# A transformer block on one core: first two key products in five parts, eight initial warm-up products, two x tiles ahead of the key weights, and new orders

## The chip, the cores and the metric

The program runs on one core of a Trainium2 chip. The core has TensorE (PE in the profile, with its weight loads as PEld), VectorE (DVE), ScalarE (ACT), GpSimd (POOL) and SyncE (SP), which here only issues DMAs. The metric is the device time of one execution in microseconds (us). Matrix products write to PSUM, which this kernel divides into four buffers of two banks each; everything else lives in SBUF.

## The reference

The input x has 2,048 rows of 640 features in bfloat16. It is normalised, goes through linear attention with 32 heads of 20 features, and then through a dense layer with 1,728 hidden features. Cut to what matters:

```python
q, k, v = split(layernorm(x) @ wqkv)                # 32 heads of 20
pq, pk  = q @ w_phi, k @ w_phi                      # per head, 20 x 20
phi_q   = concat(softmax(pq), softmax(-pq))         # 40 features; phi_k likewise
kv, z   = sum_s phi_k * v, sum_s phi_k              # over all rows
o       = (phi_q @ kv) / (phi_q @ z + 1e-6)
h       = x + o @ wo
out     = h + silu(layernorm(h) @ w1) @ w2
```

## The kernel before

The rows are cut into 16 tiles of 128 rows (t = 0 to 15). The work is written as some 620 small steps, each a Python function `op_..`, and the text `ORDER` (lines 25 to 67) lists them one after the other as words: `kp.3.0.3` calls `op_kp(3, 0, 3)`. Each engine runs its own steps in the order of this text; semaphores make it wait for what it reads and for buffers that it overwrites. Each engine takes its instructions strictly in order, so a step that waits holds up all later steps of the same engine. A DMA is issued by SP or ACT, as the last letter of its word says (`s`, `a`); a copy or product by DVE, ACT or POOL (`v`, `a`, `p`).

The steps at the start, with the lines of the profile:

- `lx.a.b`, `lk.a.b`, `lv.a.b` (L220) load tiles a to b of x, and 128-row chunks a to b of the five of the key weights wk and of the value weights wv; `lp` loads w_phi. One tile or chunk is 160 KB. `l1`, `l2`, `lh`, `lo` load the weights of the dense layer and of the output.
- `wm.n` (L254) is a product of a constant tile with n columns whose result nobody reads. Six of 512 columns stand ahead of `ORDER`, and two more stand in it.
- `wt.c` (L302) transposes wk chunk c on PE in five instructions, and `wc.c` copies it out of PSUM (L160 on DVE, L162 on ACT). `ph` (L190) spreads w_phi over a block diagonal. `fk.c` (L317) multiplies the two in six products, and `fc.c` (L162) casts the result into chunk c of Wfk: key weights with w_phi folded in.
- `st.t` (L260) takes a tile's statistics, `rs` and `rm` (L265, L269) make the scale and shift, `xn.t` (L277, L282) normalises. Tiles 0 to 3 are transposed on PE (`xt`, L288) and copied (`xc`), the others by a DMA transpose (`xd`, L295).
- `kp.t.a.b` and `vp.t.a.b` (L347) are the key and value products of tile t over chunks a to b of the five; each chunk takes two products of 320 columns. Without a and b all ten are made.
- `lq.c` (L235) loads a chunk of the query weights transposed by DMA, into the buffer that held wk, so after all `wt` have read the part that it overwrites; `gk.c` (L317) and `gc.c` fold w_phi into it.

Then `ke` (exponentials, L368), `kr` (sums, L376) and `ka` (normalisation, L384, on POOL) finish each tile's keys, `vc` casts its values, and `cc` (L406) adds them into one PSUM buffer that is held for the whole stage. `qp` and `qe` (L426, L436) make the queries. After `close`, tile by tile, `dp` (L459), `dw`, `dr` and `do` (L494) make the output of the attention, `td` transposes it by DMA, `op` (L521) multiplies with wo, `oa`, `sq`, `sa`, `sr`, `hn` and `hd` normalise and transpose it again; `up` (L595), `ua` (L617) and `yp`, `yh`, `yq` (L641, L656) are the dense layer, and `yo`, `yz`, `so`, `sz` add x and store. There is no planner at run time: the order in the text is the order on the chip.

Of the kernel before, what the change touches and what calls it, by code (L numbers as in the profile page):

```python
# [30 lines left out]
xc.1.a rs.4.2 vc.2.a vp.1 xn.5.v xn.4.v xd.5 st.7 vp.0 vc.1.a st.8 xd.4 rs.6.2 vc.3.a gk.2 st.11
vc.0.a rm.7 kp.1 lq.0 ke.0 st.9 lq.4 vp.5 ke.1 st.10 xn.6.v vp.4 xn.7.a rs.8.4 st.12 xd.6 vc.5.a
st.13 kp.5 mo vc.4.a xd.7 gc.2.a st.14 kp.4 ke.5 lo.s rm.9 xn.11.v st.15 gk.4 xn.9.a gk.0 kr.3 kp.6
rs.12.4 gc.4.a xd.9 ke.4 vp.6 rm.14 lq.3 rm.13 xn.8.v ke.6 ka.3.p kr.1 vp.7 xd.11 gc.0.a gk.1 xd.8
xn.12.v vc.7.a ka.1.p kp.7 kr.2 xn.14.a xd.12 vc.6.a vp.9 xn.13.a xn.15.v ka.2.p kr.0 gc.1.a kp.9
xd.13 vc.9.a ke.7 vp.11 xd.15 xn.10.v ka.0.p kr.5 l2.4.8.s cc.1 l1.2.s cc.3 vc.11.a l2.0.4.s cc.2
kr.6 xd.14 ke.9 gk.3 ka.5.p kp.8 gc.3.a lh.s vp.13 kr.7 ke.8 l1.1.s ka.6.p xd.10 kp.12 vc.13.a kr.4
vp.12 ka.7.p kr.9 kp.15 vc.12.a ke.12 ka.4.p kp.13 kr.8 kp.11 ka.9.p kr.12 cc.5 cc.6 ke.15 cc.7 cc.0
cc.4 ka.12.p ke.11 kr.15 kp.14 ke.13 vp.15 kr.11 ka.15.p ke.14 vp.14 vc.15.a kr.14 vp.8 ka.8.p kp.10
vc.8.a kr.13 ka.14.p qp.0.0 ke.10 vc.14.a kr.10 qp.0.2 ka.13.p qe.0.0 vp.10 qe.0.2 ka.11.p qp.1.0  # L40
vc.10.a qp.0.1 ka.10.p qe.1.0 cc.15 qe.0.1 cc.9 cc.12 cc.11 cc.14 cc.13 cc.8 cc.10 qp.1.2 km.0 close
km.1 dp.1.0 qe.1.2 dp.1.1 qp.1.1 dw.1.v dp.0.0 qe.1.1 dp.0.1 dr.1 qp.2.1 dw.0.v dp.3.0 qe.2.1 dp.3.1
dr.0 qp.3.0 dw.3.v do.0.1.p do.0.0.p td.0 dp.5.1 qe.3.0 dp.5.0 dr.3 qp.2.0 dw.5.v l1.0.s do.3.0.p
do.1.0.p do.3.1.p do.1.1.p dp.4.0 td.3 qe.2.0 dp.4.1 dr.5 op.0 dw.4.v do.5.0.p td.1 do.5.1.p qp.2.2
oa.0 dp.2.1 qe.2.2 dp.2.0 dr.4 qp.3.2 dw.2.v do.4.1.p sq.0 do.4.0.p op.1 qe.3.2 sa.0 td.4 sr.0
dp.9.1 dr.2 dp.9.0 oa.1 op.3 td.5 hn.0 sa.1 sq.1 dw.9.v do.2.1.p hd.0 qp.3.1 sr.1 hn.1 op.4 oa.3
qe.3.1 hd.1 sa.3 op.5 do.2.0.p oa.4 td.2 sq.4 dp.10.0 dp.10.1 up.0.1 dw.10.v l2.8.13.s op.2 dr.9
ua.0.1 dr.10 do.9.1.p oa.5 do.10.0.p up.0.3 oa.2 do.9.0.v dp.6.1 ua.0.3 dp.6.0 dp.8.1 sq.3 dw.6.v
td.9 up.0.0 sq.2 sr.3 sq.5 sa.4 dp.8.0 sr.4 ua.0.0 up.0.2 dw.8.v sa.2 sa.5 op.9 dr.6 ua.0.2 hn.4
do.6.0.p hd.4 sr.5 yp.1.0 oa.9 sr.2 hn.3 hn.5 hd.3 dr.8 dp.7.1 dp.7.0 hn.2 do.8.1.p yh.0.0 do.8.0.v  # L50
yp.1.1 hd.5 do.10.1.p sa.9 hd.2 do.6.1.p yp.0.0 yo.1 dw.7.v yp.0.1 dr.7 dp.11.1 do.7.0.v do.7.1.p
dp.11.0 up.1.5 yo.0 td.7 dw.11.v td.8 up.1.6 ua.1.5 td.10 dp.13.1 ua.1.6 so.0 dp.13.0 up.1.2 td.6
dw.13.v dp.15.0 dp.15.1 up.1.1 dw.15.v op.8 ua.1.1 dr.11 sq.9 op.6 ua.1.2 op.7 oa.6 dr.13 sa.6 sq.6
do.11.0.v up.1.3 oa.7 sr.6 oa.8 do.11.1.v sa.8 up.1.4 ua.1.3 sa.7 do.13.1.p sq.8 sr.9 dp.12.0 ua.1.4
dp.12.1 up.1.0 hn.9 do.13.0.v sq.7 hd.9 dw.12.v sr.7 td.11 op.10 ua.1.0 td.13 hn.6 yp.3.0 oa.10 so.1
dr.15 hn.7 dr.12 dp.14.0 dp.14.1 do.12.0.p yh.1.1 dw.14.v yp.3.1 do.15.0.p do.12.1.p sa.10 td.12
yp.5.0 sr.8 dr.14 hd.6 yp.5.1 hd.7 op.11 yo.5 yp.4.0 oa.11 hn.8 sa.11 yo.3 hd.8 op.12 do.15.1.v
do.14.0.v td.15 op.13 oa.12 so.5 sq.12 up.2.2 so.3 sq.11 up.2.0 ua.2.2 op.15 ua.2.0 up.2.6 oa.15
oa.13 yh.1.0 do.14.1.v sq.13 up.2.1 td.14 sq.15 ua.2.6 yp.2.0 ua.2.1 up.2.5 up.2.4 ua.2.5 sq.10
sr.10 up.2.3 sr.11 sa.13 hn.11 yp.4.1 ua.2.3 sa.15 sa.12 ua.2.4 sr.13 op.14 yp.9.1 oa.14 hn.10 sa.14  # L60
sq.14 hd.10 sr.12 yp.9.0 sr.14 hn.12 yo.4 yp.2.1 sr.15 hn.13 so.4 hd.12 yp.8.1 yo.2 hd.11 so.2
yp.7.1 hd.13 yh.2.1 yh.2.0 yo.9 yp.8.0 so.9 yp.7.0 up.3.3 yo.7 hn.14 hn.15 hd.14 yo.8 up.3.4 ua.3.3
hd.15 so.8 yp.6.0 ua.3.4 up.3.0 up.4.3 yp.6.1 up.4.1 yo.6 so.6 so.7 up.3.2 ua.4.1 ua.3.0 up.3.5
ua.3.2 up.4.2 ua.3.5 up.4.0 ua.4.2 up.3.1 ua.4.0 ua.4.3 up.3.6 ua.3.1 yp.15.1 ua.3.6 yp.14.1 yp.10.1
yp.14.0 yp.12.1 yp.15.0 yh.4.0 yh.3.0 yp.12.0 yp.10.0 yo.12 yo.14 yo.15 yp.11.0 so.15 so.12 so.14
yp.11.1 yh.3.1 yq.13.0 yo.11 yo.10 so.11 so.10 yq.13.1 yz.13.0 yz.13.1 sz.13.0.s sz.13.1.a
"""

@with_exitstack
def kernel(  # L70
# [181 lines left out]
    def op_wm(n=512, ps=None):  # L252
        ps = mm2() if ps is None else ps
        nc.tensor.matmul(ps[:, 0, 0:n], warm[:, 0:P], warm[:, 0:n], start=True, stop=True)  # L254
        return ps
# [462 lines left out]
```

## Time and profile before

| | |
|---|---|
| Median of 3 runs | 240.59 us (239.21 to 241.1) |
| The profiled execution's own time | 240.93 us |
| Its span, first to last instruction | 239.0 us |
| Mean granted TensorE clock | 0.999 |
| PE busy | 232.8 us |
| HBM read, written | 9.61 MB, 2.62 MB |

The span begins with the program's first instruction and leaves out what the device does around it (1.93 us in this execution). Times in the views count from the span's start. A row of a view that groups instructions gives their count, their busy time and the mean of one; the text in `<-` names what ended the engine's idle time. Matrix products are pipelined, so the distance between two of them, not the duration of one, is what a product costs.

### The profile page before, as it was taken

Reading aid. Unit: us, or ns where it says so; the run is one execution under the profiler, and the core shown is the slowest. Engines: PE = TensorE matmul, PEld = TensorE weight load, DVE = VectorE, ACT = ScalarE, POOL = GpSimd, SP = SyncE. Lnnn points to the kernel's source line nnn. Section 1 sums busy time; section 2 is a strip of 40 time slices with the busy share of each in tenths; the row PEclk is TensorE's granted clock in tenths of the full one; section 3 lists DMA queues with packets and bytes.
Section 4 is the critical chain, followed back from the end, with each engine's and each line's share of the span. In section 5 each row is a group of like instructions: output and inputs, shape, how many; then the busy total and the mean of one; then the engine's idle time right before and its main releaser. Section 6 shows DMA issues by size and latency. Waiting matters only on the chain.

```text
span 239.0 us, 5196 instructions
## 1 busy us (share of the span) xinstructions
PE 232.8 (97%) x2140; PEld 151.5 (63%) x2156; DVE 130.6 (55%) x254; ACT 104.4 (44%) x154; POOL 90.8 (38%) x167
## 2 busy tenths in 40 slices
PE   6999999999999999999999999999999999999995
PEld 2977777777574456786656467655576556757662
DVE  3679999999408998786966584430042301000043
ACT  2677998656865674661035510244510113550000
POOL 6423599999950566348201641000550000000000
PEclk9999999999999999999999999999999999999999
DMA  6995596970000264615360054401046221000022
GB/s 170 369 191 126 114 204 114 352 191 0 3 3 3 38 170 88 185 32 76 45 133 0 2 110 82 110 3 27 1 29 139 55 58 55 0 3 0 0 85 82
DMA packets 42807, 20.60 MB, mean 86 GB/s; under 512 B 34336, under 2 KB 42272, under 8 KB 42784
## 3 DMA queue, kind: packets, MB, share of 16 engines
q1 hardware_dynamic: 41984, 20.21, 36.9%
q8 instruction: 17, 0.28, 0.5%
q10 hardware_dynamic: 800, 0.06, 0.3%
q14 instruction: 6, 0.05, 0.1%
HBM read 9.61 MB, written 2.62 MB: 51 GB/s over the span
## 4 chain that ended last, share of the span: by engine, by line
PE 95%; DMA 2%; ACT 1%; issue 1%; SPq 0%; DVE 0%
PE mm L641 24%; PE mm L595 24%; PE mm L347 18%; PE mm L426 9%; PE mm L521 9%; PE mm L459 3%; PE mm L406 3%; PE mm L317 2%; DMA wk<-in_A_wqkv_dram 2%; PE mm L605 1%; PE mm L656 1%; PE mm L302 1%; ACT EqT L436 1%; PE mm L288 0%; SPq L220 0%
## 5 line engine op out<-in xcount | busy, mean ns | idle before, releaser
L641 PE MATMUL mm<-w,shT 128*128 128x320 bf16 (+2 forms) x415 | 58.6, 299 | 0.2 <-issue 0.2
L595 PE MATMUL mm<-HnT,w 128*128 128x512 bf16 (+1 forms) x316 | 58.3, 335 | 0.4
L617 ACT ACTIVATE shT<-mm 128x1024 bf16<-128x1024 f32 (+2 forms) x29 | 27.6, 964 | 59.2 <-PE mm L595 53.8
L641 PEld LDWEIGHTS <-shT 128*128 128x128 bf16 x416 | 39.7, 98 | 18.0 <-issue 1.5
L595 PEld LDWEIGHTS <-w 128*128 128x128 bf16 x325 | 31.1, 98 | 23.1 <-issue 0.3
L664 DVE TENSOR_TENSOR ob<-mm,X 128x640 bf16<-128x640 f32 x15 | 12.1, 820 | 49.9 <-PE mm L641 43.4
L347 PEld LDWEIGHTS <-XnT 128*128 128x128 bf16 x320 | 30.9, 98 | 11.7
L384 POOL TENSOR_TENSOR Ek<-Ek,Sk 128x1280 bf16<-128x1280 bf16 x16 | 37.3, 2371 | 0.0
L494 POOL TENSOR_TENSOR o<-u,rd 128x320 bf16<-128x320 f32 x23 | 16.7, 748 | 24.0 <-DVE rd L488 11.8
L436 ACT ACTIVATE EqT<-mm 128x1024 bf16<-128x1024 f32 (+1 forms) x24 | 19.7, 880 | 11.6 <-PE mm L426 11.6
L347 PE MATMUL mm<-Wfk,XnT 128*128 128x320 bf16 x160 | 24.0, 299 | 0.0
L521 PE MATMUL mm<-wo,ot 128*128 128x320 bf16 x160 | 23.7, 299 | 0.0
L347 PE MATMUL mm<-wv,XnT 128*128 128x320 bf16 x160 | 23.7, 299 | 0.0
L376 DVE TENSOR_REDUCE Sk<-Ek 128x64 f32<-128x1280 bf16 x16 | 23.1, 1444 | 0.6 <-ACT Ek L368 0.6
L426 PE MATMUL mm<-XnT,Wfq 128*128 128x512 bf16 x94 | 22.9, 379 | 0.4
L368 ACT ACTIVATE Ek<-mm 128x640 bf16<-128x640 f32 x32 | 20.3, 718 | 4.4 <-PE mm L406 2.7
L538 ACT ACTIVATE sq<-X 128x640 bf16<-128x640 bf16 x16 | 11.7, 734 | 20.6 <-DVE X L530 20.5
L530 DVE SCALAR_TENSOR_TENSOR X<-mm,X 128x640 bf16<-128x640 f32 x16 | 12.9, 814 | 14.4 <-PE mm L521 14.3
L521 PEld LDWEIGHTS <-ot 128*128 128x128 bf16 x160 | 15.5, 98 | 6.8
L426 PEld LDWEIGHTS <-Wfq 128*128 128x128 bf16 x100 | 9.3, 98 | 10.4 <-issue 0.3
L560 DVE TENSOR_SCALAR hn<-X,HM 128x640 bf16<-128x640 bf16 x16 | 7.1, 456 | 15.1 <-POOL HM L554 15.1
L260 DVE BATCH_NORM_STATS2 stats<-X 128x6 f32<-128x320 bf16 x32 | 13.7, 469 | 2.1 <-DMA X<-in_A_x_dram 2.1
(69 smaller groups left out, 199.4 us busy)
## 6 DMA issues: line engine op xcount, KB each, us to landing
out_dram<-ob SPq DMA_DIRECT2D x15, 160.0 KB, 2.0
w<-in_B_w_dram SPq DMA_DIRECT2D x3, 720.0 KB, 6.5
X<-in_A_x_dram SPq DMA_DIRECT2D x3, 640.0 KB, 9.1
w<-in_B_w_dram SPq DMA_DIRECT2D x2, 640.0 KB, 6.5
wk<-in_A_wqkv_dram SPq DMA_DIRECT2D x5, 160.0 KB, 3.9
wo<-in_A_wo_dram SPq DMA_DIRECT2D x1, 800.0 KB, 6.2
w<-in_B_w_dram SPq DMA_DIRECT2D x1, 800.0 KB, 4.7
wv<-in_A_wqkv_dram SPq DMA_DIRECT2D x1, 480.0 KB, 7.9
```

The lines of the kernel that those rows point to most:

```text
L260: nc.vector.bn_stats(stats[:, k, :], X[:, t, k * 320 : (k + 1) * 320])
L347: nc.tensor.matmul(ps[:, half, 0:320], tok(XnT[t // GT], t)[:, c, :], W[:, c, half * 320 : (half + 1) * 320], start=(c == 0), stop=(c == C ...
L368: nc.scalar.activation(Ek[:, s, :].rearrange("p (a n) -> p a n", a=2), tl["kp", t][:, :, 0:320], AF.Exp, scale=1.0 - 2.0 * s,)
L376: nc.vector.tensor_reduce(Sk[:], tl["ek", t][:].rearrange("p s (h f) -> p (s h) f", f=DH), axis=AX.X, op=ALU.add,)
L384: eng.tensor_tensor(Ek3, Ek3, tl["sk", t][:, lo:hi].unsqueeze(2).to_broadcast([P, hi - lo, DH]), op=ALU.mult,)
L426: nc.tensor.matmul(ps[:, k, :], Wfq[:, c, r * P : (r + 1) * P], XnT[g][:, c, :], start=(c == 0), stop=(c == C - 1),)
L436: nc.scalar.activation(E[:, s, rs[0] : rs[-1] + 1, :], tl["qp", g, i][:, 0 : len(rs), :], AF.Exp, scale=1.0 - 2.0 * s,)
L494: (nc.vector if eng == "v" else nc.gpsimd).tensor_tensor(tl["o", t][:, a * 320 : (a + 1) * 320].rearrange("p (h f) -> p h f", f=DH), tl["u ...
L521: nc.tensor.matmul(ps[:, half, 0:320], tl["ot", t][:, c, :], wo[:, c, half * 320 : (half + 1) * 320], start=(c == 0), stop=(c == C - 1),)
L595: nc.tensor.matmul(ps[:, i * W : (i + 1) * W], w1[:, c, fc * P : (fc + 1) * P], HnT[g][:, c, 0:W], start=(c == 0), stop=(c == C - 1), skip ...
L617: nc.scalar.activation(sh[:, a:b], tl["up", g, k][:, 0 : b - a], AF.Silu)
L641: nc.tensor.matmul(ps, shT[g][:, fc * W + i * P : fc * W + (i + 1) * P], w2[:, fc, a:b], start=first and fc == 0, stop=last and fc == FC - ...
```

## The change

The six initial warm-up products become eight. In `ORDER`:

- x tiles 2 and 3 are loaded in one DMA ahead of the key weights; x tiles 1 and 0 are loaded one by one after the first part of the value weights. The chunks of the key weights come in the order 2, 0, 3, 1, 4 (before: 2, 1, 4, 0, 3).
- The key products of tiles 3 and 2, which were made in two parts (chunks 0 to 3 and 3 to 5), are made in five parts of one chunk each. The first part of tile 3's value products now comes ahead of its key products.
- One more filler (`wm.256`) stands in the order.
- The transposed loads of the query weights come in the order 4, 0, 3, 1, 2 and closer together; the load of x tiles 8 to 12 stands between them.
- Steps move between engines: the copies `wc.2` and `wc.0` from DVE to ACT and `wc.4` from ACT to DVE; `xn.7` and `xn.9` to DVE and `xn.6`, `xn.10`, `xn.11` and `xn.15` to ACT (with their `rm`), `xn.14` to DVE; half of the normalisation of tile 6 (`ka.6.h`, `kb.6`) and the cast `vc.14` to DVE; of the halves of `do`, five go from POOL to DVE and three from DVE to POOL. The last two stores swap their queues.
- The order of nearly all other steps is new as well. What they compute is the same, and no function is changed.

```diff
 ORDER = """
-lp.a lx.3.4.s ta lk.2.3.s lk.1.2.s mk lk.4.5.s lk.0.1.s ph.p lx.2.3.s st.3 lk.3.4.s wt.2 lx.0.2.s
-lv.0.3.s wt.1 rs.3 wc.2.v lv.3.5.s wt.4 wc.1.v wt.0 lx.4.8.s mc wc.4.a fk.2 xn.3.v lx.8.12.s fk.1
-wc.0.v fc.2.a st.2 wm.512 fk.0 fc.1.a wt.3 xt.3 fc.0.a lq.1 wc.3.v fk.4 rs.2 xc.3.v wm.256 fk.3
-fc.4.a kp.3.0.3 xn.2.v fc.3.a lq.2 st.0 xt.2 kp.3.3.5 xc.2.a lx.12.16.s st.1 vp.3.0.3 ke.3 kp.2.0.3
-rs.0.2 kp.2.3.5 xn.0.v vp.2.0.3 ke.2 xn.1.v st.5 xt.0 vp.2.3.5 xc.0.a st.4 vp.3.3.5 xt.1 kp.0 st.6
...
+lp.a lx.2.4.s ta lk.2.3.s lk.0.1.s mk lk.3.4.s lk.1.2.s lk.4.5.s lv.0.3.s ph.p lx.1.2.s st.3
+lx.0.1.s wt.2 lv.3.5.s st.2 wc.2.a rs.3 lx.4.8.s wm.512 wt.0 wm.256 wt.3 wc.0.a fk.2 wc.3.v rs.2
+wt.1 fc.2.a fk.0 xn.3.v fk.3 wc.1.v mc fc.0.a xt.3 fk.1 xc.3.v wt.4 fc.1.a xn.2.v wm.256 vp.3.0.3
+lq.4 wc.4.v fc.3.a st.1 mo xt.2 kp.3.0.1 lq.0 xc.2.a kp.3.1.2 kp.3.2.3 st.0 fk.4 vp.2.0.3 fc.4.a
+lx.8.12.s rs.0.2 lq.3 vp.3.3.5 kp.3.3.4 vc.3.a kp.3.4.5 xn.0.v vp.2.3.5 lq.1 xn.1.v ke.3 st.5
+kp.2.0.1 kp.2.1.2 xt.0 lh.s kp.2.2.3 st.4 xc.0.a kp.2.3.4 xt.1 vc.2.a kp.2.4.5 lq.2 kp.0 st.6 rs.4.2
+ke.2 xn.5.v vp.0 xc.1.a xn.4.v xd.5 st.7 ke.0 kp.1 st.11 lx.12.16.s rs.6.2 vc.0.a xd.4 st.8 vp.1
+ke.1 xn.7.v st.10 gk.2 xd.7 gk.0 gc.2.a vp.5 st.9 vc.1.a lo.s gc.0.a kr.1 gk.3 rs.8.4 kp.5 gc.3.a
...
-yp.11.1 yh.3.1 yq.13.0 yo.11 yo.10 so.11 so.10 yq.13.1 yz.13.0 yz.13.1 sz.13.0.s sz.13.1.a
+yo.11 so.15 so.11 so.9 yq.13.1 yz.13.0 yz.13.1 sz.13.0.a sz.13.1.s
 """
...
-        for i in range(6):
+        for i in range(8):
             ps = op_wm(512, ps)
```

More of the change, by code (lines that the diff above doesn't have):

```diff
@@ L31 @@
[L31 to L65, printed above, removed]
@@ new lines @@
+kp.2.0.1 kp.2.1.2 xt.0 lh.s kp.2.2.3 st.4 xc.0.a kp.2.3.4 xt.1 vc.2.a kp.2.4.5 lq.2 kp.0 st.6 rs.4.2
+ke.2 xn.5.v vp.0 xc.1.a xn.4.v xd.5 st.7 ke.0 kp.1 st.11 lx.12.16.s rs.6.2 vc.0.a xd.4 st.8 vp.1
+ke.1 xn.7.v st.10 gk.2 xd.7 gk.0 gc.2.a vp.5 st.9 vc.1.a lo.s gc.0.a kr.1 gk.3 rs.8.4 kp.5 gc.3.a
+rm.10 gk.1 xn.9.v ke.5 ka.1.p vp.4 st.12 xd.9 gc.1.a st.14 kp.4 vc.5.a xn.8.v vc.4.a rm.6 st.15 xd.8
+vp.7 ke.4 st.13 kp.7 xn.6.a kr.2 rs.12.4 xn.10.a xd.6 vp.9 ke.7 rm.13 xn.12.v ka.2.p kr.4 kp.9 xd.12
@@ new lines @@
+vc.9.a vc.7.a gk.4 l2.0.4.s ke.9 vp.8 xd.10 xn.14.v ka.4.p kr.0 gc.4.a vp.6 xn.13.a vc.8.a kr.3 kp.6
+rm.11 rm.15 ka.0.p cc.2 kr.7 cc.1 ke.6 cc.4 kp.8 ka.3.p vc.6.a kr.5 xn.15.a qp.0.0 ke.8 xd.15 ka.7.p
+kr.9 xd.14 vp.12 qe.0.0 l2.8.13.s ka.5.p kr.8 kp.12 l1.1.s vc.12.a xn.11.a qp.1.0 ke.12 ka.8.p xd.11
+kr.12 kp.15 l1.0.s qe.1.0 xd.13 ka.9.p kp.10 l1.2.s l2.4.8.s cc.0 cc.7 ka.12.p ke.10 cc.3 cc.5 cc.8
+kr.10 vp.10 kp.14 vc.10.a kr.6 ka.10.p ke.15 kp.11 ke.14 kp.13 ka.6.h ke.11 kr.14 vp.15 ke.13 kr.11
@@ new lines @@
+ka.14.p qp.0.2 qp.0.1 qe.0.2 kr.13 vc.15.a ka.11.p vp.13 kr.15 vp.14 ka.13.p vc.13.a qe.0.1 kb.6
+vp.11 vc.14.v ka.15.p cc.12 vc.11.a cc.9 cc.6 cc.11 cc.10 cc.14 cc.13 cc.15 qp.1.2 km.0 close km.1
+dp.1.0 qe.1.2 dp.1.1 qp.1.1 dw.1.v dp.0.1 qe.1.1 dp.0.0 dr.1 qp.2.1 dw.0.v dp.3.1 qe.2.1 dp.3.0 dr.0
+qp.3.0 dw.3.v do.0.0.p do.0.1.p do.1.1.p td.0 dp.5.0 qe.3.0 dp.5.1 dr.3 qp.2.0 dw.5.v do.3.1.p
+do.3.0.p do.1.0.p dp.4.1 td.1 qe.2.0 dp.4.0 op.0 dw.4.v td.3 qp.2.2 oa.0 dp.2.1 qe.2.2 dp.2.0 dr.5
+sa.0 qp.3.2 dr.4 dw.2.v do.5.1.p sq.0 op.1 do.5.0.p qe.3.2 sr.0 td.5 dp.9.0 dp.9.1 dr.2 qp.3.1 hn.0
@@ new lines @@
+do.2.1.p do.2.0.v hd.0 oa.1 do.4.0.p do.4.1.p dw.9.v sq.1 td.2 op.3 sa.1 qe.3.1 sr.1 td.4 op.5 hn.1
+dr.9 hd.1 op.2 oa.5 oa.3 sa.5 op.4 do.9.1.p oa.2 up.0.3 sq.2 oa.4 dp.10.1 sa.4 sq.4 dp.10.0 up.0.0
+dw.10.v ua.0.3 sr.4 sq.5 sa.3 do.9.0.p dp.6.0 ua.0.0 dp.6.1 up.0.1 sa.2 dw.6.v td.9 sq.3 sr.3 dp.8.1
+dr.10 ua.0.1 dp.8.0 sr.2 up.0.2 dw.8.v sr.5 do.10.0.p dp.7.0 do.10.1.v ua.0.2 dp.7.1 op.9 dr.6 hn.5
+do.6.1.p hn.3 hd.5 do.6.0.p hn.2 yp.0.0 hn.4 hd.2 oa.9 yp.0.1 dw.7.v td.6 hd.3 yp.1.0 dr.8 do.8.0.v
@@ new lines @@
+hd.4 yh.0.0 dp.11.0 dp.11.1 yo.0 yp.1.1 do.8.1.v dr.7 dw.11.v do.7.1.p op.6 sa.9 up.1.0 do.7.0.v
+yo.1 td.7 oa.6 up.1.6 td.8 ua.1.0 sa.6 so.1 so.0 dp.13.0 ua.1.6 dp.13.1 td.10 op.7 dw.13.v sq.6
+up.1.3 dr.13 dr.11 oa.7 do.11.0.p dp.15.1 dp.15.0 do.13.0.v up.1.1 dw.15.v op.8 ua.1.1 dr.15 ua.1.3
+up.1.2 oa.8 sq.9 sa.8 sq.8 do.13.1.p up.1.5 sr.9 ua.1.2 sr.6 up.1.4 sa.7 ua.1.5 hn.6 hd.6 op.10
+ua.1.4 sq.7 yp.3.1 sr.7 sr.8 yp.3.0 do.11.1.p hn.8 do.15.0.p yp.5.1 do.15.1.v oa.10 hn.7 sa.10 hn.9
+dp.12.1 dp.12.0 yh.1.1 hd.9 yp.5.0 yo.3 dw.12.v td.15 yp.4.1 hd.8 dr.12 td.11 yp.4.0 do.12.1.v
@@ new lines @@
+do.12.0.v yo.5 td.12 dp.14.0 dp.14.1 yh.1.0 hd.7 dw.14.v yp.2.1 so.5 op.11 up.2.1 oa.11 yo.4 so.4
+op.12 ua.2.1 td.13 op.15 yp.2.0 oa.15 sa.15 up.2.0 yo.2 oa.12 dr.14 sa.12 do.14.0.v up.2.4 ua.2.0
+up.2.5 ua.2.4 sq.10 sq.15 sr.10 op.13 sq.12 sr.15 up.2.3 sq.11 oa.13 sa.11 do.14.1.v ua.2.5 sa.13
+hn.15 td.14 up.2.6 up.2.2 ua.2.6 ua.2.3 op.14 ua.2.2 sq.13 yp.8.1 oa.14 sa.14 sq.14 sr.12 yp.8.0
+sr.14 yp.6.1 sr.11 hn.14 hn.10 hn.12 hd.10 sr.13 yh.2.1 yh.2.0 hd.12 yp.6.0 so.3 hd.14 yp.9.1 yo.6
+hn.13 hd.15 yo.8 yp.7.0 hn.11 hd.11 yp.9.0 hd.13 so.6 up.4.0 so.8 yo.9 up.4.3 up.3.1 ua.4.3 yp.7.1
@@ L67 @@
+up.3.0 yo.7 ua.3.1 so.7 ua.4.0 so.2 up.4.1 up.3.3 ua.4.1 up.3.6 ua.3.3 up.4.2 ua.3.6 ua.3.0 up.3.4
+ua.4.2 up.3.2 ua.3.4 yp.15.0 ua.3.2 up.3.5 yp.14.0 ua.3.5 yp.15.1 yp.10.0 yh.4.0 yh.3.0 yp.12.1
+yp.12.0 yp.14.1 yo.12 so.12 yp.10.1 yp.11.1 yo.10 yo.14 yp.11.0 so.14 so.10 yh.3.1 yo.15 yq.13.0
+yo.11 so.15 so.11 so.9 yq.13.1 yz.13.0 yz.13.1 sz.13.0.a sz.13.1.s
 """
```

## The prediction

> **What bounds the kernel now.** I read the page first, then the windows, then the start on the chain of waits.
>
> ```profile
> span 239.0 us, 5196 instructions
> ...
> PE 232.8 (97%) x2140; PEld 151.5 (63%) x2156; DVE 130.6 (55%) x254; ACT 104.4 (44%) x154; POOL 90.8 (38%) x167
> ...
> PE   6999999999999999999999999999999999999995
> ...
> PE 95%; DMA 2%; ACT 1%; issue 1%; SPq 0%; DVE 0%
> ```
>
> TensorE is busy 97% of the span, only the first and last slices are thin, and 95% of the chain that ended last is PE. An order that moves PE work about inside the span has nothing to win there.
>
> ```profile
> 4.00:6.00 2.00, 1.01 (x9) 0.75 (x9) 0.88 (x3) 0.00 (x0) 1.83 (x3) 1.00 0.93 289
> ...
> 8.00:10.00 2.00, 2.00 (x19) 1.73 (x18) 1.02 (x4) 1.54 (x3) 0.77 (x2) 1.00 1.05 372
> ...
> 40.00:60.00 20.00, 19.95 (x257) 14.75 (x252) 19.62 (x22) 12.90 (x21) 20.00 (x10) 1.00 0.63 169
> ```
>
> The columns are window, length, busy time of PE, weight loads, DVE, ACT and POOL, granted clock, DMA share and GB/s. In 40 to 60 us PE has 19.95 of 20 us; half of 4 to 6 us is empty. The first 12 us decide, and the chain tells them:
>
> ```profile
> 1.71 3.95 DMA wk<-in_A_wqkv_dram
> ...
> 5.71 1.78 PE mm L302 x15
> 7.49 1.20 PE mm L317 x12
> 8.69 0.43 PE mm L254
> ...
> 9.71 0.46 PE mm L302 x5
> 10.18 0.28 PE mm L288 x5
> 10.46 0.32 PE mm L317 x6
> ...
> 11.34 0.81 PE mm L347 x6
> ```
>
> PE waits until 5.66 for the second chunk of key weights, then runs without a gap. Five transposes cost 0.59 us at 5.71 (1.78/3) and 0.28 from 10.18 on; six products of a key fold 0.60 (1.20/2), later 0.32. PE runs at half speed until about 9.9, although the window rows call the granted clock full. At 11.34 the key products start, with five weight transposes, five folds and one x transpose done.
>
> **The start, part by part.** The new order queues two x tiles (320 KB), the five wk chunks, wv's first part, x tile 1, x tile 0, then wv's second part.
>
> ```profile
> 0.79 0.40 SPq L220 DMA_DIRECT2D X<-in_A_x_dram  x1
> 1.26 1.83 SPq L220 DMA_DIRECT2D wk<-in_A_wqkv_dram  x4
> 3.60 0.43 SPq L220 DMA_DIRECT2D wk<-in_A_wqkv_dram  x1
> 4.08 0.43 SPq L220 DMA_DIRECT2D X<-in_A_x_dram  x1
> 4.55 0.96 SPq L220 DMA_DIRECT2D wv<-in_A_wqkv_dram  x2
> ...
> 9.96 3.45 SPq L235 DMA_TRANSPOSE wk<-in_A_wqkv_dram  x2
> 13.46 0.57 SPq L220 DMA_DIRECT2D X<-in_A_x_dram  x1
> ...
> 21.69 2.59 SPq L235 DMA_TRANSPOSE wk<-in_A_wqkv_dram  x2
> ```
>
> ```profile
> wk<-in_A_wqkv_dram SPq DMA_DIRECT2D x5, 160.0 KB, 3.9
> ...
> X<-in_A_x_dram SPq DMA_DIRECT2D x2, 160.0 KB, 3.1
> X<-in_A_x_dram SPq DMA_DIRECT2D x1, 320.0 KB, 7.0
> wv<-in_A_wqkv_dram SPq DMA_DIRECT2D x1, 480.0 KB, 7.9
> wv<-in_A_wqkv_dram SPq DMA_DIRECT2D x1, 320.0 KB, 8.2
> ...
> XnT<-xn SPq DMA_TRANSPOSE x12, 2.6
> ...
> wk<-in_A_wqkv_dram SPq DMA_TRANSPOSE x5, 4.0
> ```
>
> Issue plus time to landing gives a ladder over the bytes queued so far: 1,120 KB (fifth wk chunk) at 3.60+3.9 = 7.5; 1,440 KB (x tiles 0 and 1) at 4.08+7.0 = 11.1; 1,920 KB (wv's first part) at 4.55+7.9 = 12.4. The step from 7.5 to 11.1 is odd: 320 KB in 3.6 us, while the windows moved 372 GB/s, at which it needs 0.9. So part of that transfer was left behind while later ones went on, and all that came after it ended late too.
>
> ```profile
> 1.24 2.74 PE L254 MATMUL mm<-warm 128*128 128x512 bf16 x6 [1.24 <-DVE warm L132]
> 4.04 0.71 PE L302 MATMUL mm<-ident,wk 128*128 128x128 bf16 x5
> ```
>
> Eight warm-up products of 0.43 (the row at 8.69) run from 1.24 to 4.68. The two more take 0.86 of PE but nothing of the path: PE could use the first wk chunk at 4.04; with 160 KB more ahead of it, 0.43 at 372 GB/s, that is 4.5. The second lands at 5.66 now and a step later, 6.1, then. Without that cover the two would cost 0.86.
>
> Counted from there at half speed: transposes 4.68 to 5.27; one 512 filler to 5.70; wait for wk until 6.1; transposes to 6.7; a 256 filler, 0.21, to 6.9; transposes 7.5; fold 8.1; transposes 8.7; two folds 9.9. Then at full speed: x transpose 0.28, fold 0.32, transposes 0.28, filler 0.11: PE stands before the first value product (three of five chunks of tile 3) at 10.9. The copies between are off this path:
>
> ```profile
> L160 DVE COPY wTk<-mm 128x640 bf16<-128x640 bf16 x4 | 2.0, 492 | 2.9 <-PE mm L302 2.9
> L162 ACT COPY wTk<-mm 128x640 bf16<-128x640 bf16 x1 | 0.7, 692 | 4.2 <-PE mm L302 4.2
> L162 ACT CAST Wfk<-mm 128x640 bf16<-128x640 f32 x5 | 3.3, 693 | 1.1 <-PE mm L317 1.1
> ```
>
> Moving two wTk copies to ACT costs 0.2 us more each, where ACT had stood idle 4.2 us.
>
> Now the value product needs wv's first part. It stands after 1,600 KB, so the ladder puts it at 11.1 + 160/480 of 1.3 = 11.55; the plain rate after 7.5 would give 7.5 + 480/372 = 8.8. These are the two ends, and I take 11.55, since the change leaves alone the first 1,120 KB and whatever held a part back after them. PE then waits 0.65, and everything behind the value product waits with it, though kp.3's first parts have their weights. At 11.6 four folds stand where before had five at 11.34: the start is late by 0.26 plus the missing fold, 0.32: **+0.58 us**. Splitting kp into five parts adds no instruction; it lets PE use each folded chunk after its 0.69 cast, but it stands behind the wait.
>
> Is something else late next? x tiles 1 and 0 land at 12.0 and 12.4, where before had both at 11.1:
>
> ```profile
> 14.64 0.80 DVE L277 TENSOR_SCALAR xn<-X,MV,RS 128x640 bf16<-128x640 bf16 x2 [1.16 <-POOL RS L266]
> ```
>
> Tile 0 was normalised from 14.64 to 15.04, 3.9 us after landing; so at 16.3 now. PE reaches its transpose after 34 products of 0.135 (0.81/6), an x transpose and a fold: 11.6 + 4.6 + 0.6 = 16.8. Covered by 0.5, so nothing.
>
> The query-weight transposes move more. lq.4, lq.0, a 640 KB x load, lq.3, lq.1, two w2 parts, then lq.2 stand in SP's queue ahead of the transpose xd.5; before, two of them stood there. lq.4 waits for the last weight transposes (10.8). By the row at 9.96 two issues take 3.45: 14.3; the load 0.57; two more 2.59 to 3.45: 17.4 to 18.2; the two of w2 twice 0.5; lq.2 lands 4.0 after its issue, 22.4 to 23.2. Its product gk.2 follows 80 key and value products, three x transposes and a fold: 11.6 + 10.8 + 0.84 + 0.32 = 23.5. xd.5 issues 1.3 to 1.7 after lq.2, at 19.7 to 20.9, lands 2.6 later, and is used after gk.2 and gk.0 at 24.1. So 0, with 0.3 to 1.1 of cover; without it up to 2 us, if each of the five issues took the 1.7 of the slowest pair and a landing 5 us.
>
> **The rest.** DVE takes over half of one normalisation and one value cast; POOL loses 1.2 us:
>
> ```profile
> 71.50 1.10 DVE L416 TENSOR_TENSOR KVBD<-mm,maskS 128x420 bf16<-128x420 f32 x2 [8.56 <-PE mm L406]
> ...
> 31.65 32.70 POOL L384 TENSOR_TENSOR Ek<-Ek,Sk 128x1280 bf16<-128x1280 bf16 x14
> ```
>
> A full normalisation is 2.34 on POOL (32.70/14). On DVE a half has no row; between a 0.49 copy and POOL's 1.17, the cast the same. Their sum, 1.0 to 2.3, lies in the 8.56 DVE idled there. That POOL's chain starts earlier wins nothing, for PE is full. Later, five output halves go from POOL to DVE and three back, in stretches where neither fills. By the order, the PE work between filling a PSUM buffer and reusing it is 1.36 us at the shortest in the middle stages, before and after, against casts of 0.69. The shortest path from dp to op falls from 12.1 to 8.0 us of PE work for tile 2, but tile 0 has 8.3 in both. I put 0 for it all, with −0.1 to +1.0 for what the count can't see. PE's idle there, 0.05 per 20 us, bounds the gain.
>
> ```profile
> 236.47 0.36 ACTq L220 DMA_DIRECT2D out_dram<-ob  x1
> ```
>
> At the end the last two stores swap queues, 0 to +0.1.
>
> Sum: 0.58 on the profiled execution's own 240.93 (span 239.0 and 1.93 around it) is 241.5. The median shown is 0.34 below that execution, so 241.2.
>
> **Rivals.** *Values land early (faster).* If the left-behind part is that execution's accident, wv lands at 8.8. At half clock PE would start at 10.9, that is 11.2 with the fold against 11.34, 0.1 won. But the clock may rise sooner: in this trace it rose after 4.2 us without a gap (5.71 to 9.9); the new order has 1.24 to 5.7 unbroken, 4.4 us. Then all of the work after 6.1 (four times 0.28, an x transpose 0.28, four folds 1.28, two fillers 0.22) runs at full rate, 2.9 us, and waits for DVE's copies, 0.49 each, may add 0.2: 9.2, or 9.5 with the missing fold, 1.8 won. gk.2 would be due at 21.1, and its weights, 1.7 sooner too, land at 20.7 to 21.5: up to 0.4 back. That gives 238.8 to 240.5, likeliest 239.3. Against it: transposes, not products, fill 4.68 to 5.27, and the ladder.
> In the Trainium skill, "TensorE: Matmul & The Clock Gate", Part 1, the clock is released after a busy window of about 3.4 us that runs free of the kernel's start; eight products (3.44 us) would fill one only by luck, and by its Part 4 transposes don't count as busy. This trace agrees that six products (2.6 us) did not release it; that the phase varies no run here shows. By that rule the gain is 1.8 in some executions and 0.1 in others.
>
> *Late query weights (slower).* SP's issues stretch, gk.2 blocks PE, and vp.5 behind it. It decides if lq.2 lands after 23.5; at 2 us over it gives 243.2, at 1 us 242.2.
>
> *It changes nothing.* The wait for wv shrinks to the filler's length and all cancels: 240.6.
>
> **Numbers.** Forecast 0.45 (240.8 to 242.2), values early 0.33, late weights 0.15, nothing 0.07. The range 238.8 to 242.8 leaves out the worst of the late weights and a fifth of the faster case. About 1% (2.4 us) is what a measurement can tell from no change: faster needs under 238.2, a fifth of the faster case, 0.07; slower needs over 243.0, most of the late weights and a little of the forecast's tail, 0.13; the rest, 0.80.
>
> **What would show it.** Right: PE idle 0.3 to 1 us before the first L348 row (lines move by one), ended by DMA wv, at 11 to 12 us; folds of 0.60 until about 9.9; no PE gap until 60 us. Wrong: wv's first part landing within 6 us of issue, or folds of 0.32 before 8 us; a PE wait on DMA wk near 22 us would be the second rival; a wait over 0.5 us in the later windows would break the zero I put for the rest.

## The result and the profile after

| | before | after |
|---|---|---|
| Median | 240.72 us (239.18 to 241.41, 21 runs) | 239.58 us (239.1 to 240.66, 21 runs) |
| Ratio, 95% interval | | 0.9966 (0.9951 to 0.9982) |
| The profiled execution's own time | 240.93 us | 240.42 us |
| Its span | 239.0 us | 238.7 us |

The changed kernel is faster by 0.34%, about 0.8 us; the forecast was slower by about 0.6 us. The medians hide a shape: of the 21 times of the kernel before, 17 lie above 240.2 us and three at 239.2; of the 21 of the changed kernel, only five lie above 240.2. Of the profiled execution's gain, 0.51 us, only 0.27 stands in the span. The rest lies outside it: over its 21 runs the changed kernel spends 1.74 us outside the span on average, and in three series of 23, 35 and 35 runs the kernel before spends 2.00 to 2.03. No view shows what the device does there, and the forecast had nothing for it. Of the changed kernel's page, the span, busy time, PE in 40 slices and the chain by engine:

```profile
span 238.7 us, 5187 instructions
...
PE 232.9 (98%) x2143; PEld 150.8 (63%) x2159; DVE 136.3 (57%) x256; ACT 104.8 (44%) x155; POOL 88.8 (37%) x166
...
PE   7999999999999999999999999999999999999994
...
PE 93%; DVE 2%; DMA 2%; issue 1%; ACT 1%; DVEq 0%
```

PE is as busy as before; the first slice went from 6 to 7, and the chain now holds 2% of DVE. The windows and the start on the chain of waits show where (lines have moved by one):

```profile
4.00:6.00 2.00, 2.00 (x12) 1.02 (x11) 1.93 (x6) 0.55 (x1) 1.58 (x2) 1.00 0.99 334
8.00:10.00 2.00, 1.94 (x28) 1.59 (x26) 1.64 (x4) 1.75 (x4) 1.75 (x13) 1.00 1.04 389
40.00:60.00 20.00, 19.95 (x237) 13.65 (x231) 15.19 (x16) 16.26 (x25) 18.51 (x9) 1.00 0.73 220
```

```profile
1.24 3.59 PE mm L255 x8
4.84 0.58 PE mm L303 x5
...
7.12 0.39 PE mm L318 x6
7.51 0.28 PE mm L303 x5
7.79 0.63 PE mm L318 x12
8.42 0.32 PE mm L289 x5
...
9.18 1.87 DVE xn L278
...
11.09 0.45 PE mm L289 x5
```

```profile
11.09 0.45 PE L289 MATMUL mm<-ident,xn 128*128 128x128 bf16 x5 [0.48 <-DVE xn L278]
```

The wait for wk between 4 and 6 us is gone. Five transposes cost 0.58 at 4.84 and 0.28 at 7.51, and two folds 0.63 at 7.79: PE runs at full rate from about 7.1, where before it did from 9.97. (Both times are the first entries of full clock in the traces' records of the granted clock, and the rows' durations change there.) Then a stop that was not there before: PE stands 0.48 us for the normalisation of x tile 2, which is 1.87 us long (the last row, of PE's timeline). The loads, by issue and median time to landing, and the first product with the value weights:

```profile
wk<-in_A_wqkv_dram SPq DMA_DIRECT2D x5, 160.0 KB, 3.4
wv<-in_A_wqkv_dram SPq DMA_DIRECT2D x1, 480.0 KB, 5.8
```

```profile
9.64 0.97 PE L348 MATMUL mm<-wv,XnT 128*128 128x320 bf16 x6
```

The value weights, issued at 3.60, land at 9.4, and PE does not wait for them. To see where the difference stands, I took, for every PE instruction, the duration that its form has at full clock, summed those that had started by a time (warm-ups and fillers left out), and subtracted the sum from that time. At 24 us 7.91 us are lost before and 7.43 after; at the last PE instruction 17.28 and 16.83. All that this execution gains inside its span is made in the first 12 us.

### The profile page after: what moved, and what is told of

Its sections match the earlier page's. It is cut to its first block, busy times and chain, and to the rows that moved or that the text cites. A ratio compares the mean times of both kernels' runs of the same rounds, so it can differ in the third digit from the quotient of the medians.

```text
span 238.7 us, 5187 instructions
## 1 busy us (share of the span) xinstructions
PE 232.9 (98%) x2143; PEld 150.8 (63%) x2159; DVE 136.3 (57%) x256; ACT 104.8 (44%) x155; POOL 88.8 (37%) x166
## 4 chain that ended last, share of the span: by engine, by line
PE 93%; DVE 2%; DMA 2%; issue 1%; ACT 1%; DVEq 0%
PE mm L596 24%; PE mm L642 21%; PE mm L348 18%; PE mm L427 9%; PE mm L522 9%; PE mm L460 3%; PE mm L407 3%; DMA out_dram<-ob 2%; PE mm L255 2%; PE mm L318 1%; PE mm L606 1%; PE mm L657 1%; ACT EqT L437 1%; PE mm L303 1%; DVE xn L278 1%
## 5 line engine op out<-in xcount | busy, mean ns | idle before, releaser
L385 POOL TENSOR_TENSOR Ek<-Ek,Sk 128x1280 bf16<-128x1280 bf16 (+1 forms) x16 | 36.9, 2332 | 2.5 <-DVE Sk L380 1.6
L495 POOL TENSOR_TENSOR o<-u,rd 128x320 bf16<-128x320 f32 x21 | 15.7, 768 | 20.4 <-DVE rd L489 12.0
L544 POOL TENSOR_SCALAR HM<-HST 128x1 f32<-128x1 f32 x16 | 3.4, 210 | 40.0 <-DVE X L531 40.0
L561 DVE TENSOR_SCALAR hn<-X,HM 128x640 bf16<-128x640 bf16 x16 | 7.9, 525 | 12.2 <-POOL HM L555 12.2
```

The costliest lines, as they stand in the source:

```text
L385: eng.tensor_tensor(Ek3, Ek3, tl["sk", t][:, lo:hi].unsqueeze(2).to_broadcast([P, hi - lo, DH]), op=ALU.mult,)
L495: (nc.vector if eng == "v" else nc.gpsimd).tensor_tensor(tl["o", t][:, a * 320 : (a + 1) * 320].rearrange("p (h f) -> p h f", f=DH), tl["u ...
```

## Experiments

### The two warm-up products alone

```diff
-        for i in range(6):
+        for i in range(8):
```

In the kernel before:

> The kernel before with eight initial warm-up products instead of six, all else as in it. Clock theory: most runs fall from 240.72 to 239.3 to 239.9 us, and six products of a fold take 0.32 us before 9 us. Loads theory and later-order theory: 240.4 to 241.0, as before, or 0.2 more since the two products end after the first chunk of key weights has landed (4.68 against 4.04 us).

Measured: 239.54 us (239.2 to 240.16, 12 runs), ratio 0.9978 (0.9959 to 0.9996). Once more, later:

> The kernel before with eight initial warm-up products, once more, beside the others on the same chip. If the two warm-up products alone bring what the whole change brings: 239.2 to 239.8, ratio 0.995 to 0.998. If its first result was luck of that session: 240.3 or more.

Measured: 239.74 us (239.07 to 240.11), ratio 0.997 (0.9948 to 0.9992). The start on PE by the timeline (start, busy time, line, operation, count, idle time before and what ended it), first in the profile of the kernel before, then in this second run:

```profile
5.71 1.78 PE L302 MATMUL mm<-ident,wk 128*128 128x128 bf16 x15 [0.95 <-DMA wk<-in_A_wqkv_dram]
...
11.18 0.98 PE L347 MATMUL mm<-Wfk,XnT 128*128 128x320 bf16 x6
```

```profile
1.24 3.60 PE L254 MATMUL mm<-warm 128*128 128x512 bf16 x8 [1.24 <-DVE warm L132]
4.63 0.74 PE L302 MATMUL mm<-ident,wk 128*128 128x128 bf16 x5
5.59 1.40 PE L302 MATMUL mm<-ident,wk 128*128 128x128 bf16 x15 [0.22 <-DMA wk<-in_A_wqkv_dram]
6.83 0.79 PE L317 MATMUL mm<-phb,wTk 128*128 128x140 bf16 x12
...
9.62 0.98 PE L347 MATMUL mm<-Wfk,XnT 128*128 128x320 bf16 x6
```

Two folds take 0.79 of busy time at 6.83, where before they took 1.41 (1.20 on the chain); the first key product starts at 9.62 instead of 11.18, 1.56 us sooner, and the span is 1.5 us shorter. Not one of the 24 times of the two runs is above 240.2. Two instructions, and nothing else of the change, give as much as all of it. Inside the span they give more: the spans average 237.57 and 237.66 us in these two runs, against 238.02 in the 21 runs of the changed kernel and 238.20 in the ten of its repeat below, which makes up for it outside the span. Ratios of different series are to be compared with care, since 10 of 23, 9 of 35 and 11 of 35 runs of the kernel before have spans below 238.0, so its median moves with that share. The reverse, the changed kernel with six:

> The changed kernel with six initial warm-up products instead of eight, all else as in it. If its gain is the earlier rise of the clock that eight products bring, most runs go back to 240.4 to 240.9 us and the profile shows half-speed folds (0.60 us for six) until about 9 us or later. If the gain is the loads' order and the split key products, it stays within 0.3 us of the changed kernel's 239.58. If the later order makes it, it stays there too.

Measured: 241.59 us (241.2 to 241.79), ratio 1.0067 (1.0045 to 1.009), above the 240.4 to 240.9 that I had expected. PE's timeline:

```profile
1.25 2.74 PE L255 MATMUL mm<-warm 128*128 128x512 bf16 x6 [1.25 <-DVE warm L133]
4.74 0.71 PE L303 MATMUL mm<-ident,wk 128*128 128x128 bf16 x5 [0.76 <-DMA wk<-in_A_wqkv_dram]
...
7.20 0.81 PE L318 MATMUL mm<-phb,wTk 128*128 128x140 bf16 x6
```

The second x tile ahead of wk costs PE a wait of 0.76, which eight products cover, and the fold at 7.20 is still slow. PE waited another 1.09 for a transposed x tile at 27.74. Without the two products the rest of the change is a loss. And ten in the kernel before:

> The kernel before with ten initial warm-up products in place of six. Theory (an unbroken stretch of products raises the clock, and eight hardly fill one window): the clock is up by 6.7 us in the profile, the second key-weight chunk lands when they end, so they cost nothing, and the time is 239.2 to 239.6 with none above 240.5. Rival (eight are enough, and more of them stand in the way of the transposes): 239.8 to 240.2.

Measured: 239.79 us (239.14 to 240.44), ratio 0.9976 (0.9955 to 0.9997), between the two expectations; in the profile full clock from 5.81 and a span of 237.5. More than eight bring nothing more that these runs show.

### Why the kernel before has times at 239.2 and at 240.8

> The kernel before, looked at again, one of four looks. Theory (its times fall in two groups because six warm-up products raise the clock early in some executions alone): an execution with a span under 238 us shows the clock up before 8 us and key folds of 0.32 us from the first or second on; one with a span over 238.3 us shows it up after 8.5 us. Rival (the groups come from the loads, from the middle of the kernel or from its end): a short span with a late clock, or a long one with an early clock.

> The second of four looks at the kernel before, with the same expectations as the first: a span under 238 us goes with a clock that is up before 8 us, one over 238.3 us with a clock up after 8.5 us.

> The third of four looks at the kernel before, with the same expectations as the first: a span under 238 us goes with a clock that is up before 8 us, one over 238.3 us with a clock up after 8.5 us.

> The fourth of four looks at the kernel before, with the same expectations as the first: a span under 238 us goes with a clock that is up before 8 us, one over 238.3 us with a clock up after 8.5 us.

Three of these executions had full clock from 10.28, 9.59 and 10.64 us, and took 241.04, 240.87 and 241.26 us. The second had it from 4.22, with the same six products. Folds and the first products of the first execution, then of the second:

```profile
7.18 1.41 PE L317 MATMUL mm<-phb,wTk 128*128 128x140 bf16 x12
...
11.15 0.98 PE L347 MATMUL mm<-Wfk,XnT 128*128 128x320 bf16 x6
```

```profile
6.80 0.79 PE L317 MATMUL mm<-phb,wTk 128*128 128x140 bf16 x12
...
9.56 0.98 PE L347 MATMUL mm<-Wfk,XnT 128*128 128x320 bf16 x6
...
12.21 0.98 PE L347 MATMUL mm<-wv,XnT 128*128 128x320 bf16 x6 [0.85 <-DMA wv<-in_A_wqkv_dram]
```

It started 1.6 us sooner and lost 0.85 of it to value weights that had not landed: 240.42 us, with a span of 238.4. So my expectation missed (over 238.3 with an early clock), and the mechanism stands: whether six products raise the clock at once differs from execution to execution. None of the four took 239.2; that those times are early clocks without that wait is inferred.

| Profile | warm-ups | full clock from | first key or value product | span |
|---|---|---|---|---|
| before, and four more executions | 6 | 9.97; 10.28, 4.22, 9.59, 10.64 | 11.18; 11.15, 9.56, 11.09, 11.46 | 239.0; 239.0, 238.4, 238.9, 239.3 |
| changed, six warm-ups | 6 | 8.72 | 10.49 | 239.9 |
| before, eight (two runs) | 8 | 6.34, 6.45 | 9.87, 9.62 | 237.7, 237.5 |
| changed (two runs) | 8 | 7.14, 4.73 | 9.64, 8.95 | 238.7, 239.1 |

In the Trainium skill, "TensorE: Matmul & The Clock Gate", Part 1, the clock is released after a busy window of about 3.4 us that runs free of the kernel. These rows agree with a free phase: over the ten profiles with eight products whose record has an entry, the clock rose between 4.0 and 7.1 us.

The records also show why two products decide. Their full-clock entries last 228.69, 232.11 or 235.52 us, steps of 3.41, so I cut time into stretches of 3.41 us back from each rise and counted the share of each in which PE was at work, by its rows. In all 17 profiles with an entry, the stretch before the rise was filled to 81% or more, and every earlier one to 78% or less. Products alone don't part the two: they fill only 39% of one stretch that raised the clock (in the old start with the new rest, below), and 75% of one that didn't (the fourth execution above). So the prediction's premise that transposes don't count as busy is not borne out. In the profile of the kernel before, the wait of 0.95 us ahead of 5.71 leaves the stretch from 3.14 to 6.55 us at 70%; eight products shorten that wait to 0.2 to 0.6 us. The 81% and 78% are estimates, since the ends of products are modelled.

### The loads and the split

The changed kernel with the loads nearly as before:

```diff
-lp.a lx.2.4.s ta lk.2.3.s lk.0.1.s mk lk.3.4.s lk.1.2.s lk.4.5.s lv.0.3.s ph.p lx.1.2.s st.3
-lx.0.1.s wt.2 lv.3.5.s st.2 wc.2.a
+lp.a lx.3.4.s ta lk.2.3.s lk.0.1.s mk lk.3.4.s lk.1.2.s lk.4.5.s lx.2.3.s ph.p st.3 wt.2 lx.0.2.s
+lv.0.3.s lv.3.5.s st.2 wc.2.a
```

> The changed kernel with one x tile ahead of the key weights in place of two, and the first part of the value weights queued behind x tiles 0 to 2, as it was before. Theory that the loads' order matters once the clock rises early: PE waits for the value weights until about 11, where it started at 9.6, so 1.0 to 1.4 us are lost: 240.6 to 241.0. Rival, that the order of the loads is worth nothing: 239.4 to 239.8, with no wait of over 0.3 us for the value weights.

Measured: 242.01 us (240.98 to 243.81), ratio 1.0061 (1.0034 to 1.0087): worse than either expectation. Two rows of PE's timeline:

```profile
8.86 0.49 PE L318 MATMUL mm<-phb,wTk 128*128 128x140 bf16 x6 [0.77 <-DVE wTk L161]
...
10.58 0.97 PE L348 MATMUL mm<-wv,XnT 128*128 128x320 bf16 x6
```

The first value product starts at 10.58, 0.94 later than in the changed kernel's profile, but not for the value weights: DVE stood for x tile 2, which landed at 7.30, with a copy of weights queued behind. Two later waits for transposed x tiles (0.31 and 0.77 us) came on top. The new order needs its x tiles early.

With the first two key products in two parts again (`kp.3.0.3`, `kp.3.3.5`, `kp.2.0.3`, `kp.2.3.5`, each at the place of its last chunk):

> The changed kernel with the first two key products in two parts (three chunks, two chunks) in place of five. If the split into five gives PE work that it would otherwise wait for, a stop of 0.3 to 0.8 us for a folded chunk appears at 10 to 14 us and the time is 239.9 to 240.4. If the split is worth nothing, 239.4 to 239.8 and no such stop.

Measured: 239.77 us (239.03 to 241.31), ratio 0.9966 (0.9945 to 0.9987), the same ratio as the whole change, and no stop for a folded chunk. In this profile the clock was up at 4.02 and PE waited 0.64 for the value weights, so the start at 9.40 won nothing more. The split into five is worth nothing that these runs show.

### The order behind the start

Two kernels join the start of one order to the rest of the other. The changed start with the old rest (the steps after `kp.2.4.5` and `lq.2` in the old order):

> The changed kernel's order up to the last part of tile 2's key products (about 17 us), with its eight warm-ups and loads, and from there the order of the kernel before. If the gain is made in the start (clock or loads), 239.3 to 239.9 us. If the later order makes it, 240.5 to 241.0.

Measured: 241.86 us (241.11 to 243.25), ratio 1.0074 (1.0047 to 1.0101), above both expectations. The old start, up to `xt.1`, with eight warm-ups and the new rest:

> The old order up to the transpose of x tile 1, with eight warm-up products, and the new order from there. Earlier runs: the old order with eight warm-ups alone took 239.54. If the later order costs what the stop before the last stores of the changed kernel shows (about 0.15), 239.6 to 239.9. If the later order is worth something that a worse start hides in the changed kernel, 239.0 to 239.3. If it does nothing, 239.5. A value above 240 would mean that the splice itself makes a wait between 18 and 30 us.

Measured: 240.99 us (240.21 to 241.7), ratio 1.0014 (0.9993 to 1.0035). Both made waits of their own at the joint: 0.72 and 2.28 us before value products at 18.46 and 25.30 in the first; in the second, 0.59 before an x transpose at 15.32 and 0.46 before value products at 23.67. They say that neither start fits the other's rest, not what a rest is worth.

### What eats the early start in the changed kernel

The normalisation of x tile 2 took 1.86 us in the changed kernel, against the 0.44 of the same step for tile 3. The timeline of DVE and GpSimd there:

```profile
7.57 0.44 DVE L278 TENSOR_SCALAR xn<-X,MV,RS 128x640 bf16<-128x640 bf16 x1
...
9.18 1.86 DVE L278 TENSOR_SCALAR xn<-X,MV,RS 128x640 bf16<-128x640 bf16 x1
9.30 1.56 POOL L200 MEMSET Vp<- 128x32 bf16 x10
```

Ten memsets of GpSimd (the step `mo`, which the change had moved up from 25.93 us) run beside it. In the Trainium skill, "SBUF — State Buffer", section "SBUF: two separate sides", DVE and GpSimd share a pair of ports that one instruction holds alone; 1.86 against 0.44 agrees with it. (The row's start, 0.12 before the first memset, still overlaps the copy before it, which ends at 9.26.) To test it, `mo` goes up behind `mk`:

```diff
-... lk.0.1.s mk lk.3.4.s ... st.1 mo xt.2 ...
+... lk.0.1.s mk mo lk.3.4.s ... st.1 xt.2 ...
```

> The changed kernel with the ten GpSimd memsets of the value tiles moved from about 9.3 us to the place behind the mask's, at about 2.5 us, where GpSimd waits for w_phi. If these memsets hold up the normalisation of tile 2 on VectorE (1.86 us in the changed kernel, 0.44 in the kernel before), it takes 0.44 to 0.5 us again, PE's stop of 0.5 us before tile 2's transpose goes, and the time falls by 0.4 to 0.6 us to 239.0 to 239.2. If something else stretched it (the loads into SBUF at that time), it stays at 1.5 us or more and the time at 239.5 to 239.7.

The same normalisation in the timeline of that kernel:

```profile
8.81 0.48 DVE L278 TENSOR_SCALAR xn<-X,MV,RS 128x640 bf16<-128x640 bf16 x1
```

Measured: 239.75 us (239.54 to 240.34), ratio 0.9988 (0.9972 to 1.0005). The normalisation takes 0.48, PE's stop is gone, and the kernel is no faster. But this profile does not test the memsets: its clock was up at 4.58, so the normalisation began at 8.81, before 9.30, and would have missed them at their old place too. Two other kernels test them, the changed one with six warm-ups and the old start with the new rest. There the same memsets run from 9.33 to 10.89 and from 13.57 to 15.09, and a normalisation meets them:

```profile
10.04 1.03 DVE L278 TENSOR_SCALAR xn<-X,MV,RS 128x640 bf16<-128x640 bf16 x1
```

```profile
13.65 1.61 DVE L278 TENSOR_SCALAR xn<-X,MV,RS 128x640 bf16<-128x640 bf16 x1 [1.16 <-POOL RS L267]
```

In all three places it ends 0.2 us after the last memset, at 11.04, 11.07 and 15.26, which speaks for the memsets and against the loads. The stop at 15.32 in the spliced kernel above comes from it. The changed kernel again, for another profile:

> The changed kernel once more, for another profile. Theory (the warm-ups meet a clock window that runs free of the kernel, and the late normalisation meets the GpSimd memsets): if the clock is up before 6.8 us, the normalisation of x tile 2 begins before the memsets and takes 0.4 to 0.6 us, and the span is 237.3 to 238.1; if it is up at 7 us or later, the normalisation takes over 1 us and the span is 238.5 to 239. Rival (the two groups of times come from something else): a span of 238.5 to 239 with an early clock, or the reverse.

Measured: 239.99 us (239.31 to 240.82, 10 runs), ratio 0.9971 (0.9946 to 0.9996). The profiled execution had the clock up at 4.73, a normalisation of 0.49, and yet a span of 239.1, which my theory of the two groups excluded. PE and SP's queue between 18 and 34 us:

```profile
25.84 1.53 PE L348 MATMUL mm<-wv,XnT 128*128 128x320 bf16 x10 [0.73 <-DMA XnT<-xn]
...
32.13 1.53 PE L348 MATMUL mm<-wv,XnT 128*128 128x320 bf16 x10 [0.68 <-DMA XnT<-xn]
```

```profile
19.34 0.58 SPq L221 DMA_DIRECT2D X<-in_A_x_dram  x1
20.03 2.62 SPq L296 DMA_TRANSPOSE XnT<-xn  x2
22.71 0.57 SPq L221 DMA_DIRECT2D wo<-in_A_wo_dram  x1
24.96 8.45 SPq L296 DMA_TRANSPOSE XnT<-xn  x4
```

Transposes of x that stand in SP's queue behind ordinary loads (the x load at 19.34, wo at 22.71) land late: the first of the row at 20.03 at 25.79, 5.8 us after its issue, and the first of the row at 24.96 at 32.08, 7.1 after. The earlier PE starts, the sooner it meets them. So the next kernels change SP's queue: `lq.2` and `lq.4` change places, `lq.4` then goes behind `xd.7`; `lx.12.16` goes up behind `lx.8.12`; `lo` and `lh` go down behind `l2.0.4`.

```diff
-... lq.4 ... lx.8.12.s ... lh.s ... lq.2 ... xd.5 ... lx.12.16.s ... xd.7 ... lo.s ... l2.0.4.s ...
+... lq.2 ... lx.8.12.s lx.12.16.s ... xd.5 ... xd.7 lq.4 ... l2.0.4.s lo.s lh.s ...
```

> The changed kernel with other places in SP's queue alone: the query-weight transpose that is used first (chunk 2) and the one that is used last (chunk 4) change places and the latter goes behind the transpose of x tile 7; the last x load goes up behind the one before it; the loads of wo and of the last part of w2 go down behind the first w2 load. Theory (with an early clock the transposes that stand behind loads in SP's queue come too late, 0.7 to 1.7 us between 24 and 33 us, and eat the early start): no stop of PE for a DMA between 16 and 34 us, and 238.6 to 239.2. Rival (the stops there only take up slack that is lost anyway, or other ones follow): 239.4 to 239.8.

Measured: 239.4 us (239.17 to 239.76), ratio 0.9965 (0.9947 to 0.9983). Median times to landing of the transposes, first of the changed kernel's second profile, then of this kernel:

```profile
XnT<-xn SPq DMA_TRANSPOSE x12, 4.9
```

```profile
XnT<-xn SPq DMA_TRANSPOSE x12, 2.7
```

The stops are gone (from the first warm-up to 42 us PE shows no idle time that an operation ended), and no time lies above 239.76. The median missed my 238.6 to 239.2 and lies at the edge of the rival's 239.4 to 239.8. The spans average 237.62 us, as short as with eight warm-ups in the kernel before. With `mo` early and the store of tile 9 right behind its sum in addition:

> The kernel with the new places in SP's queue, and in addition the GpSimd memsets of the step mo right behind those of mk, before the late normalisation, and the store of output tile 9 right behind its sum. If each removes its cost: the normalisation of x tile 2 at 0.4 to 0.6 us whenever the clock rises, 0.1 to 0.2 less at the end, 238.4 to 239.0, and fewer times above 240. If the memsets hardly ever matter: the same time as with the new places in SP's queue alone.

Measured: 239.87 us (239.46 to 242.0), ratio 0.9986 (0.9963 to 1.001): no gain. The early memsets have little to win: of the six profiles with eight warm-ups and the new start that leave `mo` at its new place, only the first has the normalisation run into them; in the others it is over before they begin. The spans of this kernel are as short as without its two additions (medians 237.65 and 237.6 us). It loses outside the span, 2.18 us against 1.80 on average, and why stays open.

## Why the prediction was wrong

**What bounds the kernel.** Right: PE is at 98%, and what was won was won before 12 us.

**The two warm-up products.** "The two more take 0.86 of PE but nothing of the path" held: the first wk chunk landed at 4.66, before the products ended at 4.84, and with six products PE waited 0.76 for it. But I gave them no worth in the forecast, since I counted everything up to 9.9 at half speed. That term, put at nothing, is the first step that failed: the clock rises at 4.0 to 7.1 us, where with six products it rose at 8.7 to 10.6 in five profiles of six. In the kernel before that is worth 1.3 to 1.5 us of span beside its profile with a late clock. The rival "values land early" named it, with 0.33 and 239.3; it measured 239.58.

**The ladder of landings.** This is the second step that failed, and it alone made the forecast a loss: the +0.58 is its wait, at either clock. The ladder took 11.1 and 12.4 us from one execution in which part of an x load was left behind, and put the value weights at 11.55. They landed at 9.4; in the eight profiles of kernels with the new order of loads between 8.5 and 9.4. The row of that x load, in the profile before 7.0 us to landing, reads in the fourth of the further executions:

```profile
X<-in_A_x_dram SPq DMA_DIRECT2D x1, 320.0 KB, 4.6
```

Over nine profiles with the old order of loads it took 4.6 to 7.0, so the base of my ladder was the slowest of nine. I had the other end, 8.8, within 0.6 of all eight, and chose the wrong one, though I had called the step odd. With it the wait of 0.65 and the +0.58 fall: the first value product stands at 9.64, with four folds done, so 9.96 with the missing fold, 1.2 sooner than the 11.18 of the same view before.

**The rest of the start.** That x tiles 1 and 0 are covered held. The cover of 0.3 to 1.1 that I gave lq.2 and xd.5 goes with the late start that I assumed; with an early start the cover is used up, though not where the rival "late query weights" had it: not `gk.2` waits but value products, for transposes queued behind loads (1.41 us in the second profile). The step `mo` I had not costed at all at its new place: in the first profile 1.4 us on DVE, 0.48 of it a stop of PE.

**Middle and end.** My 0 (−0.1 to +1.0) holds: 0.48 us ahead at 24 us, 0.45 at the last product. At the end, where I had 0 to 0.1, DVE waits for a store's buffer:

```profile
235.09 1.03 DVE L677 TENSOR_TENSOR ob<-mm,X 128x512 bf16<-128x512 f32 x2 [1.20 <-DMA out_dram<-ob]
```

The last sums end at 236.12 against 236.44 before, so 0.32 of the 0.45 is left, and the end costs 0.13. The span keeps 0.27.

**The sum.** The two signs that I had named for "wrong" both came: the value weights within 6 us of issue (5.8) and folds of 0.32 before 8 us (0.63 for two at 7.79). What the change does, by these profiles, is to take away the executions in which the clock rises late. In time, new loads, split and orders add nothing that these runs can tell from zero; in spans they cost 0.4 to 0.6 us, which the 0.3 us less outside the span make up in part; and without the two warm-up products they lose 0.7%. The best of all is the changed kernel with SP's queue anew, 239.4 us; that it beats the other kernels near 239.6 is not shown, since their intervals overlap, but its times have the least spread of these, 0.6 us.

## What to carry over

Where a kernel's start runs at half clock, look at the clock in several executions before anything is costed on one: the durations of equal products show it, and two products that nobody reads may be worth more than a new order. A landing taken from one profile is one draw; where a ladder has an odd step, forecast from the plain rate and keep the odd one as the other end. A start that gets earlier uses up the cover of everything behind it, so ask of each transfer at what start it is still in time.

## What the runs showed of the hardware

- With eight products of 512 columns from 1.24 us, full clock came between 4.0 and 7.1 us (ten profiles); with six, at 4.2 once and between 8.7 and 10.6 in the five other profiles.
- The granted clock in the window rows reads 1.00 from the start, also where products take twice their later time; only durations, and the first entry of the clock record, show the slow start.
- PE's clock rose after a stretch of 3.41 us that was filled to 81% or more, transposes counted, and not after one filled to 78% or less (17 profiles; estimates from PE's rows).
- A DVE step of 0.44 us took 1.86, 1.03 and 1.61 where it met ten GpSimd memsets, and ended 0.2 us after the last of them each time. Where it was over before them, as with SP's queue anew (9.06 to 9.50, memsets from 9.64), it kept its 0.44.
- A DMA transpose lands 2.6 us after its issue with nothing ahead of it; the first behind a load in the same queue took 5.8 (640 KB) and 7.1 us (800 KB) in the changed kernel's second profile, 5.3 and 4.3 in its first.
